# Twelve of 48 weight pieces narrowed after the last scores instead of among them: a talking-heads attention with two expert layers on one core

## The chip, the cores and the metric

One core of one Trainium2 chip runs the whole program in one launch. The metric is device time in microseconds (us) of that launch. Of several runs the median counts; a difference of about 1% is what a measurement of this kernel can tell from none.

The engines are named as the profile names them: PE is TensorE (PEld its weight loads), DVE is VectorE, ACT is ScalarE, POOL is GpSimd, SP is SyncE, which here only issues DMAs. A "q" behind an engine's name is that engine's queue of instructions.

## The reference

An attention with mixed heads (4 batches, 12 heads, 448 positions, 64 wide), followed by two feed-forward layers over its 1792 tokens:

```python
scores = scale * np.matmul(q, k.transpose(0, 1, 3, 2))
scores = np.einsum('bhij,hg->bgij', scores, w_pre)
attn = softmax(scores)                      # row maximum taken off, sum + 1e-9
attn = np.einsum('bhij,hg->bgij', attn, w_post)
x = np.matmul(attn, v)                      # (B, H, S, D) -> (1792, 768)

h = x @ w_in                                # 768 x 1024
solu = h * softmax(h)
x = (layernorm(solu) * g_ln) @ w_out        # 1024 x 768

r = np.maximum(x @ w2_in, 0.0)              # 768 x 2048
out = (r * r) @ w2_out                      # 2048 x 768
```

The four weight matrices reach the kernel as 64-bit floats. The kernel narrows them to 32 bits itself: it takes two 32-bit words of each number, shifts and joins their bits, and zeroes what is too small for 32 bits. All further arithmetic is in 32 bits; the feed-forward products are made of three matmuls each on a high and a low part of every operand.

## The kernel before

**The attention in passes.** The queries are cut into 16 chunks (120, 120, 120 and 88 rows of each batch), and the chunks into 180 blocks of up to ten query rows. A loop over passes `s` (line 573, here from -5 to 91) handles two blocks at a time, and its stages are spread over neighbouring passes. Pass `s` issues the shuffles of pair `s+5` (line 220: DMAs on SP that bring all heads' scores of a block under each other), `pre(s+2)` (line 240: PE mixes the heads), `negmax` and `expo` of pair `s+2` (line 251 on DVE, 258 on ACT), `weigh(s+1)` (lines 268 to 271, three POOL instructions that divide the second mixing weights by the row sums) and `post(s)` (line 297: PE mixes again; it needs `weigh(s)`). `qk` (line 206) makes the scores of a later chunk, at most two heads' pairs a pass, until pass 79, which the code calls `last_qk`. `av` (line 336) multiplies a finished chunk by v, in 32 calls; the last three fall into pass 90. The order of the instructions on every engine's queue is the order of this loop: the schedule is written out by hand, and no queue overtakes.

**The first weights during the attention.** `w1pieces` (line 380) lists 48 pieces of 128 by 256 numbers: 24 of `w_in`, then 24 of `w_out`, three for each 128 rows. For one piece there is a load of 256 KB on POOL's queue (line 386), a square on ACT (80), three bit operations on DVE (83, 87, 91; `filler()` runs them, seven at a time, in passes with an `av`), a comparison and a product on POOL (100, 101), for `w_out` a scaling by `g_ln` on ACT (407) and a store of 128 KB on SP (412) into the DRAM tiles `w1iD` and `w1oD`. The pace is a budget of bytes (lines 565 to 591): what pieces, k, q, v and results move is spread evenly from pass 5 to pass 64. When all pieces are through (pass 75 by this bookkeeping), the pool `raws` closes and `wi1` opens.

**The end of the attention.** `prep_first` (line 418) brings the first layer's operands in: a load on SP (433, 438), a cast on ACT (444) and a subtraction on POOL (445) make the two parts of a block; a load runs two steps ahead of its cast, in three buffers. It takes three steps when `wi1` opens, one each in passes 80 to 84 and two each from pass 85; its last splits are in pass 88. At pass 79 the pools of q and k (`early`) and of the even chunks' scores are closed, and `wi1b` opens in their place. `h1(0)`, the first product of the first layer (line 457), begins in passes 88 and 89 and ends in pass 90 behind the last `av`. In pass 90 the last results go out by DMAs on ACT's queue (line 370).

**The first layer.** For each of 14 tiles of 128 tokens: `h1(m)` on PE, `norm1(m)` on DVE, ACT and POOL (lines 713 to 739), then `zt(m)`, PE's transposes of its result (line 753), and `out1` (767). `load_w1_out` (687) reads `w1oD` two blocks of 128 rows per tile in the first four tiles; the split casts on ACT and subtracts on POOL (692, 693). From the fourth tile on a generator, `w2stream` (line 788), narrows the second weights in another manner: a square on ACT (806), one POOL instruction that makes a mask (807), and three bit operations on DVE (831, 835, 837).

Of the kernel before, what the change touches and what calls it, by code (L numbers as in the profile page):

```python
# [7 lines left out]
F32 = mybir.dt.float32  # L8
F32R = mybir.dt.float32r
U32 = mybir.dt.uint32  # L10
I64 = mybir.dt.int64
AF = mybir.ActivationFunctionType
ALU = mybir.AluOpType
# [5 lines left out]
def kernel(  # L19
# [16 lines left out]
    nc = tc.nc  # L36
    B, D, _ = qT.shape
# [15 lines left out]
    scale = 1.0 / float(D) ** 0.5  # L53
# [19 lines left out]
    g_sb = const.tile([128, F1 // 128], F32, name="g_sb")  # L73
# [42 lines left out]
    raws = tc.tile_pool(name="raws", bufs=1, side="left", reuse_waits="tile")  # L116
# [35 lines left out]
    NP = NB // 2  # L152
# [222 lines left out]
    WP = 256  # L375
    w1raw = {}
    w1f = {}
    w1s = {}
    w1t = {}
    w1pieces = [(w1_in, w1iD, k, o) for k in range(CC) for o in range(0, F1, WP)]  # L380
    w1pieces += [(w1_out, w1oD, k, o) for k in range(F1 // 128) for o in range(0, DM, WP)]

    def load_w1(i):
        src, dst, k, o = w1pieces[i]
        t = raw_p.tile([128, WP], I64, tag="w1raw", name="w1raw", bufs=7)
        nc.gpsimd.dma_start(out=t, in_=src[k * 128:(k + 1) * 128, o:o + WP])
        w1raw[i] = t
# [22 lines left out]
    def store_w1(i):  # L410
        src, dst, k, o = w1pieces[i]
        nc.sync.dma_start(out=dst[k * 128:(k + 1) * 128, o:o + WP], in_=w1t.pop(i))

    w1i = []
    xs = {}
# [51 lines left out]
    def run(part):  # L467
        for _ in part:
            pass
# [72 lines left out]
    for c, ch in enumerate(chunks):  # L542
        if c:
            beg = (chunks[c - 1]["first"] + 1) // 2 - DS
            end = ch["first"] // 2 - DS
            for p in range(HP):
                rest = end - beg >= HP
                s = beg + rest + p * (end - beg - rest) // HP
# [13 lines left out]
    last_qk = max(s for s, js in jobs.items() for f, a in js if f is qk)  # L562
    w1at = []
    kept = 0
    kb = {load_k: 448, load_v: 384, load_q: 360, x_out: 360}
    moved = {s: sum(kb.get(f, 0) for f, a in js) for s, js in jobs.items()}
    first_w1, last_w1 = 5, 64
    share = (384 * len(w1pieces) + sum(moved.get(s, 0) for s in range(first_w1, last_w1))) / (last_w1 - first_w1)
    room = owed = begun = 0
    last_raw = None  # L570
    at_slot(2, load_const)
    lo_s = min(min(jobs), -DS)
    for s in range(lo_s, NP + 2):
# [8 lines left out]
        ready = sorted(w1t)  # L582
# [3 lines left out]
                f(*a)  # L586
        if first_w1 <= s:
            room += share - moved.get(s, 0)
        while room >= 384 and owed < len(w1pieces):
            room -= 384  # L590
            owed += 1
        for _ in range(2):
# [28 lines left out]
        for i in sorted(w1f):  # L621
            sq, t = w1f.pop(i)
# [10 lines left out]
        for i in ready:  # L633
            store_w1(i)
        kept = begun - len(fill)
        if last_raw is None and kept == len(w1pieces) and not w1t and not w1s and not w1f:
            last_raw = s
            assert s < last_qk, s
            raws.__exit__(None, None, None)
            wi1 = tc.tile_pool(name="wi1", bufs=1, side="left", reuse_waits="tile")  # L640
            wi1_p = wi1.__enter__()
            half_line(wi1_p)
            prep = prep_first()
        if s == last_qk:
            early.__exit__(None, None, None)
            sspools[0].__exit__(None, None, None)
            wi1b = tc.tile_pool(name="wi1b", bufs=1, side="left", reuse_waits="tile")
            wi1b_p = wi1b.__enter__()
        if s + DP == NP - 1:
            psb.__exit__(None, None, None)  # L650
            psh = tc.tile_pool(name="psh", bufs=1, side="left", space=PSUM, reuse_waits="tile")
            psh_p = psh.__enter__()
            h10 = h1(0)
# [8 lines left out]
        if s == NP:  # L662
            run(prep)
            run(h10)
    assert not jobs

    psa.__exit__(None, None, None)
    sspools[1].__exit__(None, None, None)
# [432 lines left out]
    low = []  # L1101
# [168 lines left out]
    for q in range(NQ):  # L1270
        p = q // NE
# [6 lines left out]
        for k, x in enumerate(seq):  # L1278
# [8 lines left out]
            if parts:  # L1287
                t, c = parts[0]
                if q == NE - 1 and (t[1] in ("p2", "p4") or t[1] in ("p7", "p3") and k < 7):
                    t = None  # L1290
                if t:
                    parts.pop(0)
                    split_xc(*t, c)
                    i = ORDER.index(t[1]) + 2
# [76 lines left out]
```

## Time and profile before

| | us |
|---|---|
| three runs | 1110.02, 1102.11, 1110.64 |
| median | 1110.02 |
| the profiled execution | 1105.38 |
| its span, first to last instruction | 1103.60 |

The span is cut into 40 slices, and a digit is the busy share of a slice in tenths. The attention fills the first 14 slices (to about 395 us), the first layer the next nine, the second the rest.

```profile
PE   7889888988899899999999999999999999999998
PEld 3556555655656687989999998999999999999998
DVE  2556666877685626788887526677656843444444
ACT  4556556767676726444443446444334655444432
POOL 2746788897684836665564338666535766666630
PEclk8899899999999999999999999999999999999999
DMA  6868778788676634565754736455455431111102
```

A wait is read as "who waited <- for whom: us in total, times, longest"; "issue" is idle time in which the engine waited for nothing that the profile shows. The clock column is the granted TensorE clock as a share of full speed, DMA the busy share of the core's 16 DMA engines.

### The profile page before, as it was taken

How to read it: one execution, taken by the hardware profiler on the slowest of the kernel's cores; microseconds unless marked ns; L12 is line 12 of the kernel's file. 1: busy time of each engine (PE TensorE's matmuls, PEld its weight loads, DVE VectorE, ACT ScalarE, POOL GpSimd, SP SyncE). 2: the span in 40 equal slices, each digit the busy share in tenths (PEclk: the TensorE clock that was granted, in tenths of full speed). 3: DMA queues.
4: the chain of work that ended last, by engine and by line, in shares of the span. 5: the costliest groups of instructions: out<-in, count | busy, mean ns of one | idle time of the engine just before them, and what ended most of it. 6: DMA issues, size and time to landing. Idle time of an engine off the chain costs nothing.

```text
span 1103.6 us, 30919 instructions
## 1 busy us (share of the span) xinstructions
PE 1043.0 (95%) x12560; PEld 890.0 (81%) x12560; DVE 680.4 (62%) x1217; ACT 562.0 (51%) x1171; POOL 673.4 (61%) x872
## 2 busy tenths in 40 slices
PE   7889888988899899999999999999999999999998
PEld 3556555655656687989999998999999999999998
DVE  2556666877685626788887526677656843444444
ACT  4556556767676726444443446444334655444432
POOL 2746788897684836665564338666535766666630
PEclk8899899999999999999999999999999999999999
DMA  6868778788676634565754736455455431111102
GB/s 176 212 179 239 207 220 260 219 259 244 202 225 196 180 99 127 166 195 167 210 159 158 229 120 181 135 157 172 143 200 192 161 129 58 58 58 58 58 29 100
DMA packets 115918, 180.33 MB, mean 163 GB/s; under 512 B 24224, under 2 KB 87328, under 8 KB 115776
## 3 DMA queue, kind: packets, MB, share of 16 engines
q1 hardware_dynamic: 100788, 128.66, 38.1%
q0 software_dynamic: 12608, 47.77, 14.5%
q10 hardware_dynamic: 2380, 1.93, 0.6%
q8 instruction: 99, 1.62, 0.6%
q14 instruction: 43, 0.35, 0.1%
HBM read 101.63 MB, written 38.14 MB: 127 GB/s over the span
## 4 chain that ended last, share of the span: by engine, by line
PE 73%; issue 7%; DMA 7%; POOL 6%; ACT 4%; DVE 4%; SPq 0%; ACTq 0%; POOLq 0%; DVEq 0%
PE ps_y L1184 19%; PE ps_h L1113 16%; PE ps_o L767 9%; PE ps_h L457 7%; PE ps_ring L336 6%; PE ps_ring L297 6%; PE ps_pre L240 5%; PE ps_ring L206 5%; DMA sdst<-ssrc 3%; ACT ssrc L213 1%; POOL ti L1041 1%; DMA ra<-w2iD 1%; DMA wraw<-w1iD 1%; ACT e L258 1%; DMA w2oD<-nt 1%
## 5 line engine op out<-in xcount | busy, mean ns | idle before, releaser
L1184 PE MATMUL ps_y<-to,gt 128*128 128x384 f32 x1332 | 241.9, 336 | 2.5 <-POOL to L1049 1.8
L1184 PEld LDWEIGHTS ps_y<-to,gt 128*128 128x128 f32 x1332 | 233.7, 188 | 4.8 <-POOL to L1049 2.1
L1113 PE MATMUL ps_h<-xc,ti 128*128 128x448 f32 x1080 | 225.1, 362 | 0.6 <-ACT h L1129 0.6
L1113 PEld LDWEIGHTS ps_h<-xc,ti 128*128 128x128 f32 x1080 | 201.6, 187 | 13.2 <-ACT h L1129 1.0
L297 PEld LDWEIGHTS ps_ring<-w,e 60*64 60x64 f32 (+1 forms) x5760 | 101.9, 137 | 70.8 <-issue 42.4
L316 DVE COPY at<-ps_ring 128x420 f32<-128x420 f32 x156 | 87.8, 611 | 94.9 <-PE ps_ring L297 94.7
L1195 DVE TENSOR_TENSOR y<-ps_y,y 128x768 f32<-128x768 f32 x97 | 92.3, 954 | 76.9 <-PE ps_y L1184 76.5
L807 POOL TENSOR_SCALAR nt<-nt 128x256 f32<-128x256 f32 x96 | 112.0, 1166 | 43.9 <-ACT nt L806 37.8
L297 PE MATMUL ps_ring<-w,e 60*64 60x60 f32 (+2 forms) x5760 | 110.3, 221 | 29.8 <-issue 23.9
L213 ACT COPY ssrc<-ps_ring 128x896 f32<-128x896 f32 x92 | 82.1, 908 | 95.7 <-PE ps_ring L206 88.8
L258 ACT ACTIVATE e<-ps_pre,nm 128x448 f32<-128x448 f32 x180 | 113.3, 640 | 23.3 <-DVE nm L251 23.1
L767 PE MATMUL ps_o<-zt,w1o 128*128 128x384 f32 (+1 forms) x720 | 120.7, 326 | 1.4 <-ACT o L775 1.2
L457 PE MATMUL ps_h<-w1i,xs 128*128 128x512 f32 x504 | 118.1, 391 | 0.7 <-POOL xs L707 0.6
L767 PEld LDWEIGHTS ps_o<-zt,w1o 128*128 128x128 f32 x720 | 116.9, 189 | 2.1 <-ACT o L775 1.6
L251 DVE TENSOR_REDUCE nm<-ps_pre 128x1 f32<-128x448 f32 x180 | 102.9, 611 | 16.9 <-PE ps_pre L240 16.9
L457 PEld LDWEIGHTS ps_h<-w1i,xs 128*128 128x128 f32 x504 | 93.9, 188 | 20.3 <-POOL xs L707 1.5
L1041 POOL TENSOR_TENSOR ti<-ra,ti 128x384 fp32r<-128x384 f32 x56 | 60.2, 1083 | 78.3 <-ACT ti L1040 77.9
L1126 DVE TENSOR_TENSOR gt<-h,gt 128x448 fp32r<-128x448 f32 x64 | 50.6, 790 | 90.2 <-ACT gt L1131 85.5
L206 PE MATMUL ps_ring<-k,q 64*64 64x448 f32 x752 | 98.3, 560 | 6.8 <-ACT ssrc L213 2.9
L240 PE MATMUL ps_pre<-sdst,wpre_bd 64*64 64x448 f32 (+1 forms) x720 | 97.8, 575 | 6.7 <-issue 5.5
L806 ACT ACTIVATE nt<-nraw 128x256 f32<-128x256 f32 x96 | 40.7, 432 | 121.6 <-DMA w2iD<-nt 47.8
L336 PEld LDWEIGHTS ps_ring<-at,v 128*64 128x64 f32 x1536 | 77.0, 140 | 31.6 <-PE ps_pre L240 9.9
(108 smaller groups left out, 1474.0 us busy)
## 6 DMA issues: line engine op xcount, KB each, us to landing
sdst<-ssrc SPq DMA_DIRECT2D x166, 210.0 KB
nraw<-in_moe_w_in_dram SPq DMA_DIRECT2D x48, 256.0 KB
nraw<-in_moe_w_out_dram SPq DMA_DIRECT2D x48, 256.0 KB
ra<-w2iD POOLq DMA_DIRECT2D x32, 384.0 KB, 4.4
ro<-w2oD POOLq DMA_DIRECT2D x32, 384.0 KB, 4.0
w1raw<-in_moe_w_in_dram POOLq DMA_DIRECT2D x24, 256.0 KB, 6.0
w1raw<-in_moe_w_out_dram POOLq DMA_DIRECT2D x24, 256.0 KB, 6.3
w2iD<-nt SPq DMA_DIRECT2D x48, 128.0 KB
```

The costliest lines, as they stand in the source:

```text
L206: nc.tensor.matmul(out=ps[64 * u:64 * u + 64, e, 0:S], lhsT=qq[c][64 * e:64 * e + 64, p * n + u * half:p * n + u * half + 64], rhs=k[64 * ...
L213: (nc.vector.tensor_copy if dve else nc.scalar.copy)(ssrc[c][:, p:H:HP, :], ps[:, :, 0:S])
L240: nc.tensor.matmul(out=ps[b][64 * u:64 * u + 64, 0:S], lhsT=wpre_bd[64 * r:64 * r + m], rhs=ds[b][64 * r:64 * r + m], start=True, stop=True,)
L251: nc.vector.tensor_reduce(out=nm, in_=pres[s][b][:, 0:S], op=ALU.max, axis=AX.X, negate=True)
L258: nc.scalar.activation(out=e, in_=pres[s][b][:, 0:S], func=AF.Exp, bias=nms.pop((s, b)), scale=1.0, accum_out=sms[s][:, b:b + 1])
L297: nc.tensor.matmul(out=ps[64 * c:64 * c + 64, u, i0:i0 + ng * RH], lhsT=e[64 * u:64 * u + m, o:o + 64], rhs=w[64 * u:64 * u + m, b, g0:g0 ...
L336: nc.tensor.matmul(out=ps[64 * e:64 * e + 64, 0, q * 120:q * 120 + n], lhsT=t[:, g] if j < NJ else t[:, e, p], rhs=at[c][:, j * H + (g if ...
L457: nc.tensor.matmul(out=ps[:, u], lhsT=t[:, a, cc], rhs=w1i[cc][:, w, u * 512:(u + 1) * 512], start=(cc == 0 and a == 0 and w == 0), stop=( ...
L767: nc.tensor.matmul(out=ps[:, 0:width], lhsT=w1o[k][:, w, cc * 128:(cc + 1) * 128], rhs=zT[:, a, k, 0:width], start=(k == 0 and i == 0), st ...
L807: nc.gpsimd.tensor_scalar(out=t, in0=t, scalar1=2.0**-30, scalar2=2.0 - 2.0**-23, op0=ALU.is_ge, op1=ALU.mult)
L1113: nc.tensor.matmul(out=bank[b][:, 0:HT], lhsT=t[:, w, c], rhs=xc[xn][:, a, c], start=(first and j == 0 and c == 0 and i == 0), stop=(j == ...
L1184: nc.tensor.matmul(out=ps[:, u - u2[0], 0:DM // 2], lhsT=gt[:, a, f, o:o + 128], rhs=w[:, v, f, u * (DM // 2):(u + 1) * (DM // 2)], start= ...
```

## The change

The budget of the attention's passes counts 36 pieces (`NW`) instead of 48; it still ends at pass 64, so the 36 are spread over the same passes. The other twelve, all of `w_out` (the last four blocks of 128 rows), are narrowed by a generator, `tail_w1`, in a pool of its own that opens behind `wi1b` at pass 79. The generator takes one step in each pass from 80 to 89, four in pass 90, one in pass 91 and the rest behind the loop, always before the step of `prep_first` of the same pass. Its first step issues four loads, its second two masks; each of the twelve steps after that issues the load four pieces on, the mask two pieces on, the three bit operations of one piece, and the scaling and the store of the piece before. It narrows in the manner of `w2stream`; loads and stores are both on SP. With fewer pieces `raws` closes at pass 72 instead of 75.

```diff
+    NW = len(w1pieces) - 12
...
+        def load(i):
+            if i in todo:
+                src, dst, k, o = w1pieces[i]
+                raws[i] = pool.tile([128, WP], I64, tag="traw", name="traw", bufs=5)
+                nc.sync.dma_start(out=raws[i], in_=src[k * 128:(k + 1) * 128, o:o + WP])
...
+        def mask(i):
+            if i in todo:
+                t = ts[i] = pool.tile([128, WP], F32, tag="tt", name="tt", bufs=6)
+                nc.scalar.activation(out=t, in_=words(i)[1].bitcast(F32), func=AF.Square)
+                nc.gpsimd.tensor_scalar(
+                    out=t, in0=t, scalar1=2.0**-30, scalar2=2.0 - 2.0**-23, op0=ALU.is_ge, op1=ALU.mult
+                )
+
+        def scaled():
+            for i in ready:
+                k = w1pieces[i][2]
+                nc.scalar.activation(out=ts[i], in_=ts[i], func=AF.Copy, scale=g_sb[:, k:k + 1])
+
+        def store():
+            while ready:
+                i = ready.pop(0)
+                src, dst, k, o = w1pieces[i]
+                nc.sync.dma_start(out=dst[k * 128:(k + 1) * 128, o:o + WP], in_=ts.pop(i))
+
+        a = todo[0]
+        for i in range(4):
+            load(a + i)
+        yield True
+        mask(a)
+        mask(a + 1)
+        yield True
+        for i in todo:
+            load(i + 4)
+            mask(i + 2)
+            low, high = words(i)
+            bits = ts[i].bitcast(U32)
+            stt = nc.vector.scalar_tensor_tensor
+            stt(out=bits, in0=high, scalar=3, in1=bits, op0=ALU.logical_shift_left, op1=ALU.bitwise_and)
+            scaled()
+            stt(out=bits, in0=high, scalar=0xC0000000, in1=bits, op0=ALU.bitwise_and, op1=ALU.bitwise_or)
+            stt(out=bits, in0=low, scalar=29, in1=bits, op0=ALU.logical_shift_right, op1=ALU.bitwise_or)
+            store()
+            raws.pop(i)
+            ready.append(i)
+            yield True
+        scaled()
+        store()
...
-    share = (384 * len(w1pieces) + sum(moved.get(s, 0) for s in range(first_w1, last_w1))) / (last_w1 - first_w1)
+    share = (384 * NW + sum(moved.get(s, 0) for s in range(first_w1, last_w1))) / (last_w1 - first_w1)
...
-        if last_raw is None and kept == len(w1pieces) and not w1t and not w1s and not w1f:
+        if last_raw is None and kept == NW and not w1t and not w1s and not w1f:
...
             wi1b_p = wi1b.__enter__()
+            tail = tc.tile_pool(name="tail", bufs=1, side="left", reuse_waits="tile")
+            tail_steps = tail_w1(tail.__enter__())
+        elif s > last_qk:
+            for _ in range(4 if s == NP else 1):
+                next(tail_steps, None)
...
     assert not jobs
+    run(tail_steps)
+    tail.__exit__(None, None, None)
```

## Rows read from the trace of the kernel before

**Rows 1.** Busy time in four stretches; columns: PE, PEld, DVE, ACT, POOL, clock, DMA, GB/s.

```profile
60.00:300.00 240.00, 207.80 (x5366) 137.50 (x5360) 164.93 (x357) 155.75 (x367) 183.50 (x330) 0.97 0.78 228
300.00:345.00 45.00, 40.02 (x1110) 28.05 (x1108) 32.99 (x74) 33.00 (x82) 33.25 (x61) 1.00 0.69 200
345.00:376.00 31.00, 29.72 (x908) 21.31 (x906) 19.69 (x39) 21.64 (x51) 18.74 (x32) 1.00 0.67 196
376.00:395.00 19.00, 15.87 (x409) 12.76 (x402) 9.95 (x22) 9.86 (x22) 16.88 (x22) 0.91 0.58 170
```

**Rows 2.** Waits of PE, 60 to 300 us: us in total, times, longest.

```profile
PE ps_ring L297 <- issue: 17.9, 13, 3.1
PE ps_pre L240 <- issue: 5.5, 2, 3.3
```

**Rows 3.** Waits of PE, 300 to 345 us.

```profile
PE ps_ring L297 <- issue: 3.0, 2, 2.0
```

**Rows 4.** Timeline of PE, one stop inside a group of line 297.

```profile
336.99 1.08 PE L297 MATMUL ps_ring<-w,e 60*64 60x60 f32 x58
340.09 0.31 PE L297 MATMUL ps_ring<-w,e 60*64 60x30 f32 x6 [2.02 <-issue]
```

**Rows 5.** DMA queues, 337.5 to 338.9 us: packets, MB, share.

```profile
q8 instruction: 1, 0.02, 4.2%
```

**Rows 6.** Waits of PE, 345 to 376 us.

```profile
PE ps_ring L297 <- POOL w L271: 0.7, 1, 0.7
PE ps_ring L297 <- issue: 0.4, 1, 0.4
```

**Rows 7.** Waits of PE, 376 to 395 us.

```profile
PE ps_ring L297 <- issue: 1.9, 1, 1.9
PE ps_ring L297 <- POOL w L271: 1.3, 2, 0.7
```

**Rows 8.** Timeline where the attention ends; the releaser stands in brackets.

```profile
392.35 0.39 POOL L271 TENSOR_TENSOR w<-wpost_bd,sm 128x120 f32<-128x120 f32 x1
...
392.79 1.13 PE L297 MATMUL ps_ring<-w,e 60*64 60x60 f32 x64 [0.51 <-POOL w L271]
...
403.89 2.02 ACTq L370 DMA_DIRECT2D xD<-xt  x3
406.09 1.23 DVE L717 TENSOR_REDUCE nm<-ps_h 128x1 f32<-128x1024 f32 x1 [10.94 <-PE ps_h L457]
...
414.25 0.86 PEld L753 LDWEIGHTS ps_tr<-id_sb,e 128*128 128x128 f32 x8 [0.46 <-ACT e L738]
```

**Rows 9.** Groups of the whole trace: both narrowings, of the first and second weights.

```profile
L807 POOL TENSOR_SCALAR nt<-nt 128x256 f32<-128x256 f32 x96 | 112.0, 1166 | 43.9 <-ACT nt L806 37.8
...
L835 DVE SCALAR_TENSOR_TENSOR nt<-nraw,nt 128x256 uint32<-128x256 uint32 x96 | 64.4, 671 | 2.5
...
L837 DVE SCALAR_TENSOR_TENSOR nt<-nraw,nt 128x256 uint32<-128x256 uint32 x96 | 51.6, 537 | 2.8
...
L831 DVE SCALAR_TENSOR_TENSOR nt<-nraw,nt 128x256 uint32<-128x256 uint32 x96 | 44.8, 467 | 7.6 <-POOL nt L807 7.6
L100 POOL TENSOR_SCALAR w1sq<-w1sq 128x256 f32<-128x256 f32 x48 | 41.3, 860 | 4.1
L806 ACT ACTIVATE nt<-nraw 128x256 f32<-128x256 f32 x96 | 40.7, 432 | 121.6 <-DMA w2iD<-nt 47.8 <-DMA w2oD<-nt 33.6 <-DVE nt L837 11.3
...
L101 POOL TENSOR_TENSOR w1t<-w1t,w1sq 128x256 f32<-128x256 f32 x48 | 35.0, 729 | 4.0
```

**Rows 10.** The splits on POOL at the attention's end, 361 to 395.3 us: busy, mean ns | idle before.

```profile
L445 POOL TENSOR_TENSOR w1i<-wraw,w1i 128x512 fp32r<-128x512 f32 x12 | 15.2, 1276 | 2.9 <-ACT w1i L444 1.5 <-DMA sdst<-ssrc 0.9 <-DMA wraw<-w1iD 0.5
```

**Rows 11.** Timeline of SP's queue in the passes after the last scores.

```profile
362.10 1.33 SPq L433 DMA_DIRECT2D wraw<-w1iD  x1
```

**Rows 12.** The page's DMA issues: KB each, us from issue to landing.

```profile
ra<-w2iD POOLq DMA_DIRECT2D x32, 384.0 KB, 4.4
...
w1raw<-in_moe_w_out_dram POOLq DMA_DIRECT2D x24, 256.0 KB, 6.3
```

More of the change, by code (lines that the diff above doesn't have):

```diff
@@ L412, in store_w1, with tail_w1, words @@
         nc.sync.dma_start(out=dst[k * 128:(k + 1) * 128, o:o + WP], in_=w1t.pop(i))
+    def tail_w1(pool):
+        todo = range(NW, len(w1pieces))
+        raws, ts, ready = {}, {}, []
+        def load(i):
[3 more added lines that the diff above has]
+                nc.sync.dma_start(out=raws[i], in_=src[k * 128:(k + 1) * 128, o:o + WP])
+        def words(i):
+            pair = raws[i].bitcast(U32).rearrange("p (n two) -> p n two", two=2)
+            return pair[:, :, 0], pair[:, :, 1]
+        def mask(i):
[37 more added lines that the diff above has]
+        store()
     w1i = []
@@ L588 @@
             room += share - moved.get(s, 0)
-        while room >= 384 and owed < len(w1pieces):
+        while room >= 384 and owed < NW:
             room -= 384
```

## The prediction, made before the change was run

> **What bounds the kernel now.** I read the page first, then the busy times by stretch, the waits of PE stretch by stretch, the chain of waits, and the timeline from the last scores to the first layer. Up to 345 us the attention and the first weights run together; from 345 us the weights are through; at 376 us the passes with two splits each begin [rows 1]. From 60 to 345 us PE is idle for 32.2 + 5.0 = 37.2 of 285 us [rows 1], and most of that is "issue": 23.4 us before 300 us in the two largest rows [rows 2] and 3.0 us behind it [rows 3], 26.4 together. These are stops inside a group: 58 of the 64 matmuls of one `post` start, then nothing for two microseconds, then the last six [rows 4]. In that stop the instruction queue moves one packet of 16 KB [rows 5], and the other long stops have such a packet too. So I read them as PE's own instructions arriving late, among data that keeps the DMA engines 78% busy [rows 1].
>
> Behind 345 us it looks otherwise. With the DMA engines 67% busy such stops cost 0.4 us in 31 us [rows 1, 6]. From 376 us on POOL is busy for 16.88 of 19 us, more than PE [rows 1], and PE waits for `weigh` as well as for issue [rows 7]: the last `post` starts right after POOL's last `weigh` [rows 8]. POOL alternates `weigh`, which the next `post` needs, with the splits. The end of the attention is thus POOL's, and everything earlier is PE's with stops.
>
> **What the attention's passes get back.** Twelve pieces fewer are a quarter of the first weights: 12 x 384 KB = 4.7 MB of the 240 x 228 + 45 x 200 = 63.7 MB that move from 60 to 345 us [rows 1], and on POOL 12 x (0.86 + 0.73) = 19 us [rows 9], beside their loads' issue. POOL, DVE and ACT have idle time there, and hardly a wait of PE for them is long, so what counts is PE's idle time. Issue costs 23.4 / 240 = 0.098 us per us before 300 us, 3.0 / 45 = 0.067 while the last pieces drain, and (0.4 + 1.9) / 50 = 0.046 with no first weights [rows 1 to 3, 6, 7]. By the last of these the first weights cause 26.4 - 0.046 x 285 = 13.3 us, and a quarter is 3.3; by the middle one 26.4 - 0.067 x 285 = 7.3, a quarter 1.8; if all of it were theirs, 6.6. I take 3.5. Of PE's other idle time, 37.2 - 26.4 = 10.8 us, a quarter would be 2.7; I take 2. Sum: 5.5 us back, bounds 1.8 and 9.3.
>
> A rule of the Trainium skill speaks against the larger part. "Runtime: NRT & Kernel Launch", section "Instruction fetch mechanics", says that instructions come in 16 KB blocks by a DMA queue of their own, and that this is hidden because dispatch is slower than the refill. The block size agrees with rows 5; that it is hidden doesn't agree with the stop in rows 4. By the rule 3.5 of the 5.5 us would fall away, which is the third rival.
>
> **What the end of the attention pays on POOL.** The new masks are the instruction of line 807, 1.17 us each [rows 9]; with a gap of 0.08 us ahead of each, as POOL's old comparisons had (4.1 us idle over 48) [rows 9], 1.25 us. Two are issued in pass 81, one in each of passes 82 to 87, all ahead of `weigh(89)`, the last that `post` waits for: 8 x 1.25 = 10.0 us. What can hide them is POOL's idle time ahead of the splits, 2.9 us [rows 10], so the bounds are 7.1 and 10.0. Part of that idle time is a wait for ACT's casts, which also get work, and 0.9 us of it falls into pass 80, before any mask. I take 8.5. The masks of pieces 8 and 9 come behind `weigh(89)` and delay the last splits, which `h1(0)` needs only after 6 us of `av`: nothing.
>
> **On the other queues.** DVE's three operations, 0.47 + 0.67 + 0.54 = 1.67 us a piece [rows 9], fit into its idle time (it is busy for 19.69 of 31 and 9.95 of 19 us) [rows 1]; so does ACT's square of 0.43 and one scaling. SP gets twelve loads and twelve stores. The first four loads stand ahead of pass 80's `prep_first` load and pass 81's shuffles; one load issue took 1.33 us [rows 11], so the shuffles are some 5 us later. They have three passes until `pre` needs them, and by then POOL's masks have moved `pre` back as far: I take nothing, bounds 0 and 2. A store waits for its scaling on ACT, and the loads of `prep_first` queue behind it; that is the second rival. New traffic also brings back stops of PE; much of that falls into waits for POOL. I take 1.0, bounds 0 and 3.
>
> **What the first layer pays.** In pass 90 the masks of pieces 10 and 11 are queued behind the last copies and four DMA issues on ACT, which end at 403.89 + 2.02 = 405.9 us [rows 8]. From there, on the old clock: square 0.43 (406.4), mask 1.17 and a gap (407.6), three DVE operations of piece 10 (409.3), and of piece 11 (411.0), whose mask is ready by then. All these are queued ahead of the row maximum of `norm1(0)`, which started at 406.09, the moment that `h1(0)` was done [rows 8]. It comes 4.9 us later. PE makes `h1(1)` meanwhile, but that cover is used up already: `zt(0)` waited 0.46 us for the end of `norm1(0)` [rows 8]. From there on PE has no pause to catch up in. I take 4.9, bounds 3.2 (one piece's 1.67 us less, if DVE has done piece 10 by then) and 6.1 (one more mask of 1.17 in the way). The first layer's tiles may lie where the new pool was and wait for its last stores; the trace of before can't show that: 0, at most 4 by the nearest landing of 4.4 us [rows 12].
>
> **Sum.** Against the profiled execution, 1105.4: -5.5 + 8.5 + 1.0 + 4.9 = +8.9, so 1114.3. That execution lies 4.6 us under the median of the runs, which spread over 8.5 us, and 3.3 over the fastest. I stay close to the sum and forecast 1115 us: slightly slower, by less than the 1% (11 us) that a measurement of this kernel can tell from no change.
>
> **The rivals.**
> First, the stops vanish out of proportion and the change is no loss. For it: with 67% busy DMA engines they were nearly gone, 0.4 / 31 = 0.013 per us [rows 1, 6]. 4.7 of 63.7 MB are 7.4%, which takes 78% to 72%, or 0.06 of the 0.11 on the way to 67%: 55% of 23.4 - 0.013 x 240 = 20.3 us, so 11.2, with 2.7 of the other waits 13.9 back. POOL hides the 2.9 it can (7.1), the first layer pays 4.9: 1105.4 - 13.9 + 7.1 + 4.9 = 1103.5. It decides from about 13 us back. Against it: from 300 to 345 us the engines were 69% busy and stops cost 0.067 all the same.
>
> Second, SP and the DMA engines take over at the end, and the kernel is slower for certain. From 361 to 395 us about 15 x 196 + 19 x 170 = 6.2 MB move [rows 1]; twelve loads and seven stores add 4.0. At the 228 GB/s of the loaded stretch [rows 1] 10.2 MB want 45 us, where the old 34 us and POOL's 8.5 make 42.5. A load of 256 KB took 6.3 us to land in the loaded stretch, against 4.4 us for 384 KB later [rows 12], 2 us more. In passes 85 to 88 ACT's casts wait for such loads with the next exponentials behind them: 4 x 2 = 8 us on top, 1122.3. PE, waiting longer, may also be granted less clock; it was 0.91 there already [rows 1]. Against it: the pieces' traffic is spread over more passes than these four.
>
> Third, the stops are not of the traffic but of PE's own dense groups, and don't change; only 1 or 2 us of other waits come back. Then 1105.4 - 2 + 8.5 + 1.0 + 4.9 = 1117.8. For it: in the last 19 us, with 58% busy DMA engines and no first weights, they cost 1.9 / 19 = 0.10 per us again [rows 1, 7]. The rule of the skill named above would make it so as well, by another road. Against it: a fall from 0.098 to 0.013 as the pieces end.
>
> **How the numbers follow.** The forecast gets 0.45 (1108 to 1120), the first rival 0.20 (1097 to 1107), the second 0.18 (1120 to 1130), the third 0.17 (1114 to 1122). The range is 1100 to 1126: it leaves out the lower end of the first rival and the upper half of the second, under 0.2 together. Slower by over 1%, from 1121 us: 0.15 of the second, 0.07 of the third, 0.08 of the forecast, as the runs may lie above a profile by as much as they did before: 0.30. Faster by over 1%, under 1099 us: 0.08, all of the first. Within 1%: 0.62.
>
> **What would show it.** In the profile after: PE's waits for issue from 60 to 345 us fall from 26.4 to some 23 us and the passes to pass 80 end 5 or 6 us sooner; behind it POOL is busy without a gap, PE's waits for `weigh` rise from 2.0 to about 8 us, the last `post` stands 2 to 5 us later than 392.79; the row maximum of `norm1(0)` starts some 5 us after the end of `h1(0)`, its releaser a tail operation on DVE, and `zt(0)` waits as long. From then on both kernels keep step. Wrong would be: `weigh` not last at the end of the attention (then SP, DMA or nothing is), stops of PE down by more than a third or unchanged, or `norm1(0)` starting with `h1(0)`'s end.

## The result: slower by about 1%, with the profile after

The change makes the kernel slower: 1119.51 us in the median of six runs (1117.60 to 1127.92) against 1109.99 in six of the kernel before beside them. The medians differ by 9.5 us; the ratio on record for these runs is 1.0111 with a 95% interval of 1.0067 to 1.0155, which is some 12 us (7.4 to 17.2). The forecast was 1115 in a range of 1100 to 1126; the sign and the range hold, and the loss lies on the border between "same" and "slower" at 1%.

The execution that was profiled after took 1122.39 us (span 1120.6), 17.0 more than the one profiled before, so this pair lies further apart than the medians. First the busy times by stretch, with the columns of [rows 1]; the last stretch ends later, as the attention does:

```profile
60.00:300.00 240.00, 208.87 (x5366) 141.34 (x5364) 155.01 (x327) 148.90 (x348) 163.90 (x302) 0.96 0.74 212
300.00:345.00 45.00, 40.37 (x1085) 28.26 (x1080) 29.69 (x67) 29.92 (x73) 27.22 (x53) 0.96 0.71 206
345.00:376.00 31.00, 25.60 (x780) 18.30 (x780) 19.92 (x40) 22.02 (x53) 17.16 (x27) 0.97 0.60 181
376.00:408.00 32.00, 23.71 (x564) 18.61 (x558) 24.98 (x43) 16.61 (x40) 29.35 (x36) 0.82 0.66 199
```

Up to 345 us the removed work is plain to see on POOL (163.90 us for 183.50 in the first stretch) and in the traffic (212 GB/s for 228), but PE is busy hardly longer, 208.87 us for 207.80. From 345 us PE loses: 25.60 of 31 us for 29.72 [rows 1]. Then POOL is busy for 29.35 of 32 us.

Second, whom PE waited for, from 60 to 345 us, to be held against [rows 2, 3]:

```profile
PE ps_ring L297 <- issue: 12.2, 12, 3.1
PE ps_pre L240 <- issue: 8.8, 3, 3.6
PE ps_ring L206 <- issue: 4.8, 2, 2.6
PE ps_ring L336 <- issue: 3.8, 2, 3.4
```

These are 29.6 us; all of PE's issue waits in the same stretch of before were 28.8 (the prediction's 26.4 is the rows of [rows 2, 3] alone). This one execution gave nothing back. From 345 to 408 us, where before had 2.0 us of waits for `weigh` [rows 6, 7]:

```profile
PE ps_ring L297 <- POOL w L271: 4.1, 1, 4.1
...
PE ps_ring L297 <- POOL w L271: 7.0, 2, 4.6
PE ps_ring L297 <- DVE at L316: 1.3, 1, 1.3
```

POOL's groups from 361 to 408 us show what was added: the splits of [rows 10] are the same in number and nearly in length (1.32 us for 1.28), and the masks stand beside them.

```profile
L504 POOL TENSOR_TENSOR w1i<-wraw,w1i 128x512 fp32r<-128x512 f32 x12 | 15.6, 1315 | 1.6 <-ACT w1i L503 1.0
L434 POOL TENSOR_SCALAR tt<-tt 128x256 f32<-128x256 f32 x9 | 10.0, 1106 | 2.8 <-ACT tt L433 1.3 <-DMA traw<-in_moe_w_out_dram 1.0
```

Last, the timeline where the attention ends, with the events of [rows 8] (in after the row maximum is line 783 and the transposes are line 819):

```profile
406.04 1.13 PE L297 MATMUL ps_ring<-w,e 60*64 60x60 f32 x64
...
417.15 2.00 ACTq L370 DMA_DIRECT2D xD<-xt  x3
...
419.20 0.43 ACT L433 ACTIVATE tt<-traw 128x256 f32<-128x256 f32 x1 [2.15 <-issue]
...
419.72 2.46 POOL L434 TENSOR_SCALAR tt<-tt 128x256 f32<-128x256 f32 x2 [9.38 <-ACT tt L433]
...
423.13 0.42 DVE L465 SCALAR_TENSOR_TENSOR tt<-traw,tt 128x256 uint32<-128x256 uint32 x1
...
423.47 1.22 DVE L783 TENSOR_REDUCE nm<-ps_h 128x1 f32<-128x1024 f32 x1
...
431.70 1.25 PEld L819 LDWEIGHTS ps_tr<-id_sb,e 128*128 128x128 f32 x8 [4.66 <-ACT e L804]
```

The last `post` starts at 406.04 for 392.79, 13.3 us later. `h1(0)` is done at 419.3, but the row maximum waits for the tail's last bit operation, until 423.47, and the transposes wait 4.66 us for 0.46. From the first transposes to the last instruction both kernels take the same: 688.9 us after, 689.4 before. So the 17.0 us are: 1.1 up to pass 79 (its row maximum starts at 359.3 for 358.2), 12.1 from there to the last `post`, 4.2 at the first layer, and 0.4 less in the rest.

### The profile page after: what moved, and what is told of

Its sections match the earlier page's. It is cut to its first block, busy times and chain, and to the rows that moved or that the text cites. A ratio compares the mean times of both kernels' runs of the same rounds, so it can differ in the third digit from the quotient of the medians.

```text
span 1120.6 us, 30899 instructions
## 1 busy us (share of the span) xinstructions
PE 1050.3 (94%) x12560; PEld 898.4 (80%) x12560; DVE 686.9 (61%) x1217; ACT 562.9 (50%) x1171; POOL 663.4 (59%) x848
## 3 DMA queue, kind: packets, MB, share of 16 engines
q0 software_dynamic: 11648, 44.62, 13.3%
q10 hardware_dynamic: 2380, 1.93, 0.6%
## 4 chain that ended last, share of the span: by engine, by line
PE 51%; POOL 4%; issue 3%; DMA 2%; DVE 1%; ACT 1%; ACTq 0%; SPq 0%; POOLq 0%
PE ps_y L1250 18%; PE ps_h L1179 15%; PE ps_o L833 10%; PE ps_h L516 7%; POOL ti L1107 1%; DMA ra<-w2iD 1%; PE ps_tr L819 1%; POOL w1o L759 1%; POOL s L1087 1%; DMA nraw<-in_moe_w_in_dram 1%; POOL to L1115 1%; DVE st L792 0%; DVE e L789 0%; DMA w1oraw<-w1oD 0%; ACT e L786 0%
## 5 line engine op out<-in xcount | busy, mean ns | idle before, releaser
L297 PEld LDWEIGHTS ps_ring<-w,e 60*64 60x64 f32 (+1 forms) x5760 | 104.4, 140 | 70.4 <-issue 32.2
L873 POOL TENSOR_SCALAR nt<-nt 128x256 f32<-128x256 f32 x96 | 112.1, 1168 | 42.1 <-ACT nt L872 36.1
L516 PE MATMUL ps_h<-w1i,xs 128*128 128x512 f32 x504 | 120.5, 397 | 0.0
L240 PE MATMUL ps_pre<-sdst,wpre_bd 64*64 64x448 f32 (+1 forms) x720 | 102.6, 583 | 9.7 <-issue 8.8
```

The costliest lines, as they stand in the source:

```text
L240: nc.tensor.matmul(out=ps[b][64 * u:64 * u + 64, 0:S], lhsT=wpre_bd[64 * r:64 * r + m], rhs=ds[b][64 * r:64 * r + m], start=True, stop=True,)
L297: nc.tensor.matmul(out=ps[64 * c:64 * c + 64, u, i0:i0 + ng * RH], lhsT=e[64 * u:64 * u + m, o:o + 64], rhs=w[64 * u:64 * u + m, b, g0:g0 ...
L516: nc.tensor.matmul(out=ps[:, u], lhsT=t[:, a, cc], rhs=w1i[cc][:, w, u * 512:(u + 1) * 512], start=(cc == 0 and a == 0 and w == 0), stop=( ...
L873: nc.gpsimd.tensor_scalar(out=t, in0=t, scalar1=2.0**-30, scalar2=2.0 - 2.0**-23, op0=ALU.is_ge, op1=ALU.mult)
```

## The experiments

One table for all of them. "To pass 79" is the start of that pass's row maximum; "end" is from there to the last `post`; "late" is by how much the row maximum of `norm1(0)` starts behind the end of `h1(0)`; "stops" are all issue waits of PE from 60 to 345 us. These four are of one profiled execution each. The ratio to the kernel before, with its interval, is the one on record for the runs beside it; it differs a little from the quotient of the medians, which is 1.0086 for after.

```
kernel                         to pass 79   end   late  stops  ratio [95%]
before                              358.2  34.6   0.0   28.8   1
before, a second profile            357.6  35.7   0.0   30.6
before, a third profile             355.1  33.5   0.0   27.9
after                               359.3  46.7   4.2   29.6   1.0111 [1.0067, 1.0155]
e1  tail left out                   351.4  36.1   0.0   21.4   0.9926 [0.9892, 0.9961]
e2  36 pieces left out              353.9  34.8   0.0   25.1   0.9912 [0.9874, 0.9949]
e3  masks on DVE                    356.9  43.1   3.5   20.2   1.0050 [1.0021, 1.0078]
e4  last pieces a pass sooner       358.3  45.7   0.1   32.0   1.0064 [1.0029, 1.0098]
e5  transfers alone, shared buffers 356.9  50.6   0.0   28.4   1.0110 [1.0072, 1.0148]
e6  arithmetic alone                357.8  46.2   4.4   20.6   1.0087 [1.0059, 1.0115]
e9  transfers alone                 355.5  43.7   0.0   25.1   0.9987 [0.9948, 1.0026]
e8  reordered, masks on POOL        354.6  43.9   0.1   27.1   1.0049 [1.0022, 1.0077]
e7  reordered, masks on DVE         354.6  40.2   0.0   26.2   1.0013 [0.9980, 1.0046]
e10 as e7, last pieces before av    351.7  41.6   0.0   23.2   0.9967 [0.9934, 1.0000]
```

PE's time in the end is either its own work or a wait. The second table parts it, from the busy times and PE's waits in that stretch of the same profiles; the work is the same in all of them. "Shuffles" are waits of line 240 for the shuffles' DMAs, "others" are waits for issue, ACT and DVE, "clock" is the mean granted TensorE clock.

```
kernel                               end   busy  weigh  shuffles  others  clock
before                              34.6   30.2    1.9       0      2.3   0.95
before, a second profile            35.7   31.1    4.4       0      0.2   0.95
before, a third profile             33.5   28.0    5.5       0      0     1.00
after                               46.7   33.0   11.1       0      2.6   0.85
e1  tail left out                   36.1   30.5    5.6       0      0     0.91
e2  36 pieces left out              34.8   29.9    3.7       0      1.3   0.95
e3  masks on DVE                    43.1   34.0    9.2       0      0     0.84
e4  last pieces a pass sooner       45.7   32.2   13.5       0      0     0.85
e5  transfers alone, shared buffers 50.6   37.7    7.9       4.7    0.2   0.83
e6  arithmetic alone                46.2   33.9    6.2       0      6.0   0.85
e9  transfers alone                 43.7   33.6    5.7       3.0    1.2   0.88
e8  reordered, masks on POOL        43.9   32.9    8.6       2.3    0     0.88
e7  reordered, masks on DVE         40.2   31.8    3.9       2.4    2.0   0.92
e10 as e7, last pieces before av    41.6   32.1    6.2       2.5    0.8   0.92
```

From e1 to after the end grows by 10.6 us: 5.5 in waits for `weigh`, 2.6 in other waits, and 2.5 in PE's own work, which runs at a lower clock.

My theory was the prediction's: the masks on POOL make the end longer, the queue order of pass 90 makes the first layer late, and the attention's passes give a few microseconds back. The rivals were that SP and the DMA engines make the end longer, and that PE's stops have nothing to do with the pieces.

**The tail left out (e1).** Edit: the generator is never made, so twelve pieces are not narrowed at all, and the first layer reads the blocks that are there.

```diff
-            tail = tc.tile_pool(name="tail", bufs=1, side="left", reuse_waits="tile")
-            tail_steps = tail_w1(tail.__enter__())
-        elif s > last_qk:
-            for _ in range(4 if s == NP else 1):
-                next(tail_steps, None)
```

> The twelve last pieces are left out altogether (36 are narrowed; the first layer's last four weight blocks are read from the first four). What the attention's passes get back by themselves is then seen without the tail. If the stops of PE don't follow the pieces (the trace of the changed kernel: waits for issue from 60 to 300 us 25.4 us against 25.2 before): the row maximum of pass 79 stands at 358 +- 3 us, the last post at 393 +- 3, and the time is within 3 us of the kernel before. If the prediction's sum was right and the one profile was an unlucky one: pass 79 some 5 us sooner than 358, and 1104 to 1106 us against 1110.

Measured: 0.9926 (0.9892 to 0.9961), 8.2 us under before (4.3 to 12). The end takes 36.1 us, against 33.5 to 35.7 in the three profiles of before, and nothing is late. Pass 79 stands at 351.4, 6.8 us sooner than in the first profile of before: of the two branches expected it is the second, and further than it said. So nearly all of the longer end and all of the late first layer are the tail's.

**A quarter of the pieces (e2).** As e1, and 24 more pieces are left out of the attention's passes.

```diff
-    NW = len(w1pieces) - 12
+    NW = len(w1pieces) - 36
```

> Only the first twelve of 48 pieces are narrowed in the attention, no tail; 36 pieces are left out, and the first layer reads blocks that are there. If PE's stops come of the first weights' traffic: waits for issue from 60 to 345 us fall from 29 us to 10 or less, and the kernel is 15 to 20 us faster than before. If they are PE's own: they stay above 20 us, and the kernel is faster by 5 us or less, by the waits for POOL, DVE and ACT alone.

Measured: the same time as e1 within the intervals, 0.9912 (0.9874 to 0.9949), or 9.8 us under before (5.7 to 14). From 60 to 345 us it has less traffic and much less work on POOL (columns of [rows 1]):

```profile
60.00:345.00 285.00, 251.68 (x6632) 169.33 (x6628) 161.15 (x327) 171.36 (x393) 140.34 (x288) 0.97 0.65 181
```

Before, by the same view, the DMA engines were busy for 0.76 at 223 GB/s and POOL for 216.75 us. Yet the stops are there still:

```profile
PE ps_ring L297 <- issue: 19.9, 13, 4.4
PE ps_ring L336 <- issue: 4.1, 4, 2.1
```

With one more of 1.1 that is 25.1 us. The stops stay above 20 us, but the gain is more than the "5 us or less" expected for that case. They don't follow the traffic down; with it at 0.65, just under the 0.67 [rows 1] at which they cost 0.4 us in 31 [rows 6], they cost 25.1 us in 285.

**Before, twice more (b1, b2).** No edit; two more profiles of the kernel before, to see how far the stops scatter.

> The kernel before, unchanged, for a second profile of its attention passes. Ten profiles of kernels with 36 pieces there have the row maximum of pass 79 between 351.4 and 359.3 us, 355.7 in the mean; the one profile with 48 has 358.2. If 36 pieces give back what the medians say (7 us without a tail): 358 to 366, with waits for issue from 60 to 345 us as scattered as in the others (20 to 32 us). If the pieces give nothing back and the medians come from elsewhere: 352 to 359.

> The kernel before once more, a third profile, with the same two expectations: 358 to 366 if the twelve pieces cost the attention's passes some 7 us, 352 to 359 if they cost nothing.

Measured: 30.6 and 27.9 us of stops, pass 79 at 357.6 and 355.1. With 48 pieces the three profiles have 29.1 us of stops on the mean. Ten kernels have 36 pieces in the attention's passes and the same instructions there; their profiles run from 20.2 to 32.0 us, 25.4 on the mean, and pass 79 from 351.4 to 359.3, on the mean 355.7 for 357.0 with 48. Both new profiles fall into the branch by which the pieces give nothing back. But a single profile can't show a gain of four microseconds here; the profile of after was among the worst of the ten. The three profiled executions of before were also quick ones, 1104.8 us on the mean, some 4 us under that kernel's medians (1108.1 to 1110.0), while the ten lay 1.5 us over the medians of theirs. With these 5.6 us added to the 1.3, pass 79 would come some 7 us sooner; this is an estimate, and it takes the whole scatter to lie ahead of pass 79.

The kept traces also say what the stops hang on. In the 14 profiles PE has 261 issue waits from 60 to 345 us, and all 261 end 1.15 to 1.9 us after the end of a packet of the instruction queue q8; the one of [rows 4] ends 1.4 us after it. Of all moments in that stretch 14% lie so, and of PE's 220 other waits 39. So I read the stops as PE waiting for its instructions, though no run varied that alone. The traffic of data does not show in the packets: there are 52 of them in that stretch of before and 53 in e2, with a median of 1.06 us each in both.

**Masks on DVE (e3).** POOL loses the masks, DVE gains them, all else stays.

```diff
-                nc.gpsimd.tensor_scalar(
-                    out=t, in0=t, scalar1=2.0**-30, scalar2=2.0 - 2.0**-23, op0=ALU.is_ge, op1=ALU.mult
-                )
...
+            nc.vector.tensor_scalar(
+                out=ts[i], in0=ts[i], scalar1=2.0**-30, scalar2=2.0 - 2.0**-23, op0=ALU.is_ge, op1=ALU.mult
+            )
```

> As the changed kernel, but the twelve masks are made by DVE just ahead of the bit operations instead of by POOL. If POOL's masks ahead of weigh are what the end of the attention pays: PE's waits for weigh behind 345 us fall from 11 us to 4 or less, the last post stands 6 to 9 us sooner than the 406 of the changed kernel, and the time is 6 to 9 us below it. If it is the landing of the new loads and the queue on SP and ACT: no more than 2 us.

Measured: 1.0050 (1.0021 to 1.0078), and an end of 43.1 us. On DVE a mask takes 0.41 us instead of 1.1 (group of line 459 in this kernel, 355 to 412 us):

```profile
L459 DVE TENSOR_SCALAR tt<-tt 128x256 f32<-128x256 f32 x10 | 4.1, 414 | 0.0
```

Of the 10.6 us that the tail adds to the end of e1, only 3.6 went with POOL's masks, and the median fell by 4.3 us where 6 to 9 were expected. PE still waits for `weigh`, POOL in its turn waits for ACT's casts, and those wait for the first layer's loads. The waits of PE, POOL and ACT from 358 to 407 us:

```profile
PE ps_ring L297 <- POOL w L271: 9.2, 3, 3.7
...
POOL w1i L504 <- ACT w1i L503: 6.7, 3, 3.2
...
ACT w1i L503 <- DMA wraw<-w1iD: 7.8, 5, 4.2
```

Before, that last wait was 4.4 us in the same stretch, and in e1, without a tail, 6.5; so the loads' landing by itself explains little. ACT is also busier, 28.2 us of the end for 22.0 in e1, with the tail's squares and scalings. There is a cause beside POOL's masks; this run does not say which.

**The last pieces a pass sooner (e4).** Three steps in pass 89 and two in pass 90, so that the last squares and masks don't stand behind pass 90's results.

```diff
-            for _ in range(4 if s == NP else 1):
+            for _ in range(2 if s == NP else 3 if s == NP - 1 else 1):
```

> As the changed kernel, but three steps of the tail are taken in pass 89 and two in pass 90, so that the last two squares stand ahead of the last copies and result DMAs on ACT. If the order of ACT's queue in pass 90 is what makes the first layer start late: the row maximum of norm1(0) starts within 0.5 us of the end of h1(0) (4.2 us behind it in the changed kernel), and the time is 3 to 5 us below the changed kernel's, less what two masks earlier on POOL cost. If the rest of the tail's work on DVE is what is late: no change.

Measured: 1.0064 (1.0029 to 1.0098). The row maximum starts with the end of `h1(0)` and the transposes wait 0.55 us, as before the change:

```profile
416.36 2.02 ACTq L370 DMA_DIRECT2D xD<-xt  x3
...
418.64 1.23 DVE L783 TENSOR_REDUCE nm<-ps_h 128x1 f32<-128x1024 f32 x1 [4.58 <-PE ps_h L516]
...
426.81 0.86 PEld L819 LDWEIGHTS ps_tr<-id_sb,e 128*128 128x128 f32 x8 [0.55 <-ACT e L804]
```

The gain is not the whole 4.2 us: the last `av` now waits 1.0 us for DVE, which has the earlier bit operations in its queue, and from the last `post` to the end of `h1(0)` it takes 14.5 us instead of 13.3. The median fell by 3.8 us; the intervals overlap, so the row shows it and the medians only agree. The end stays long, at 45.7 us.

**The arithmetic alone (e6).** No load and no store of the tail; its squares, masks, bit operations and scalings run on a tile of zeros, and the result goes nowhere.

```diff
-        for i in range(4):
-            load(a + i)
+        raw = pool.tile([128, WP], I64, name="traw")
+        nc.vector.memset(raw.bitcast(F32), 0.0)
+        for i in todo:
+            raws[i] = raw
```

> As the changed kernel, but the tail moves no data: squares, masks, bit operations and scalings work on one zeroed tile, and loads and stores of the twelve pieces are left out. From the row maximum of pass 79 to the last post: by POOL's ledger 34.6 or 36.1 plus 7 to 10, so 43 to 46; if the transfers are the cost, 38 or less. The first layer still starts 4 us late (norm1(0) behind the end of h1(0)), as those two squares stand where they stood.

Measured: an end of 46.2 us, 10.1 more than e1, with the DMA engines busy for only 0.46 of it. The arithmetic by itself makes nearly the whole longer end. The POOL group of the masks within that end:

```profile
L434 POOL TENSOR_SCALAR tt<-tt 128x256 f32<-128x256 f32 x9 | 9.8, 1084 | 0.8 <-DMA sdst<-ssrc 0.2
```

Nine masks keep POOL busy for 9.8 us, about as long. But the run takes the squares, scalings and bit operations along, so it prices all the arithmetic and not POOL's share alone: PE's waits for `weigh` are only 6.2 us here, 4.4 are put down to ACT, and ACT's exponentials wait 10.1 us for DVE's row maxima, where e1 has 4.5. e8 and e7 below part the masks from the rest.

**The transfers alone (e5, then e9).** e5 has the tail's loads and stores and no arithmetic, but stores straight out of the loads' buffers.

```diff
+        def plain(i):
+            src, dst, k, o = w1pieces[i]
+            nc.sync.dma_start(out=dst[k * 128:(k + 1) * 128, o:o + WP], in_=raws.pop(i).bitcast(F32)[:, 0:WP])
```

> As the changed kernel, but the tail only moves data: each of the twelve pieces is loaded and its first words are stored, with no instruction of the tail on ACT, DVE or POOL (the narrowing of these pieces is left out). Measure: from the row maximum of pass 79 to the last post, 34.6 us in the kernel before, 36.1 without a tail, 46.7 in the changed kernel. If POOL's masks and the waits that they make are the cost: 37 or less. If the transfers on SP and the DMA engines are: 43 or more, and ACT's waits for the loads of the first layer's weights at 7 us or more. Both in part: 38 to 42.

Measured: an end of 50.6 us, longer than after itself. That came from the experiment: a later load needs the buffer of an earlier store, and SP's queue stood still for it with the first layer's loads behind. The waits of SP's queue and of ACT, 355 to 410 us:

```profile
SPq L424 <- DMA w1oD<-traw: 20.5, 6, 4.9
...
ACT w1i L495 <- DMA wraw<-w1iD: 24.8, 10, 6.9
```

So it does not price the transfers of the change. e9 stores from a tile of zeros instead, so that no load waits for a store:

```diff
+        zero = pool.tile([128, WP], F32, name="tz")
+        nc.vector.memset(zero, 0.0)
...
+            nc.sync.dma_start(out=dst[k * 128:(k + 1) * 128, o:o + WP], in_=zero)
```

> The transfers alone once more: the twelve loads as in the change, and twelve stores of a tile of zeros, so that no load waits for a store and no store for a load (the narrowing of the twelve pieces is left out). From the row maximum of pass 79 to the last post: 36.1 us without a tail, 46.1 with its arithmetic alone, 46.7 with both. If the transfers cost nothing where POOL is last: 36 to 38, and 1100 to 1104 us. If they alone cost as much as the arithmetic does, each hiding the other: 43 or more. By the run with the masks on DVE (43.2 with the transfers) I expect 39 to 42.

Measured: an end of 43.7 us, 7.6 more than e1, where 39 to 42 was expected; it meets the branch "43 or more". Waits of PE, POOL and ACT, 355 to 410 us:

```profile
PE ps_ring L297 <- POOL w L271: 5.7, 3, 3.9
PE ps_pre L240 <- DMA sdst<-ssrc: 3.0, 2, 2.5
PE ps_ring L297 <- issue: 1.2, 1, 1.2
...
POOL w1i L499 <- ACT w1i L498: 9.2, 7, 3.7
...
ACT w1i L498 <- DMA wraw<-w1iD: 14.3, 10, 3.3
```

The second rival's chain is there: ACT's casts wait 14.3 us for their loads and POOL 9.2 for the casts, where e1 has 6.5 and 2.4. But it does not reach PE, whose waits for `weigh` are no longer than in e1:

```profile
PE ps_ring L297 <- POOL w L271: 5.6, 4, 3.1
```

What PE loses is 3.0 us of waits for the shuffles, which share SP's queue and the DMA engines with the new transfers, 1.2 of a stop, and 3.1 in its own work, at a mean clock of 0.88 for 0.91. Arithmetic 10.1 and transfers 7.6 give 10.6 together: each hides most of the other. That fits e3, which got only 3.6 us back.

**Reordered (e8, e7).** All work is done. The tail's step stands behind the step of `prep_first`, a store comes a step later than before, a scaling at the end of its step, squares a pass later, and the last pieces are spread over passes 88 to 90 (2, 3 and 2 steps). e8 leaves the masks on POOL, e7 has them on DVE.

```diff
-        elif s > last_qk:
-            for _ in range(4 if s == NP else 1):
-                next(tail_steps, None)
...
+            for _ in range({NP - 2: 2, NP - 1: 3, NP: 2}.get(s, 1)):
+                next(tail_steps, None)
```

> As the run before it, but the masks on POOL again, as in the change. If POOL's masks count by themselves: 3 to 8 us more than that run, on the way from pass 79 to the last post. If the order of the loads and stores was the whole cost: the same within 2 us.

> All twelve pieces done, but arranged by what the runs so far say: masks on DVE, the tail's step behind that of the first layer's operands in each pass, the squares a pass later than the first loads, a store a step behind its scaling, and two, three and two pieces in passes 88, 89 and 90, where ACT, DVE and POOL wait for PE. If the cost of the tail is where it stands in the queues: from pass 79 to the last post 37 to 40 us, norm1(0) within 1 us of the end of h1(0), and 1101 to 1106 us, below the kernel before (1108.1) and the changed one. If moving 4 MB there costs the same whatever the order: 43 us or more and 1110 or more.

Measured: ends of 43.9 and 40.2 us, nothing late, ratios of 1.0049 (1.0022 to 1.0077) and 1.0013 (0.9980 to 1.0046). The two differ in the masks' engine alone: 3.7 us of the end, 1.9 us behind the last `post`, and 4.8 us of the medians. PE's waits for `weigh` from 355 to 410 us, e8 first, then e7:

```profile
PE ps_ring L297 <- POOL w L271: 8.6, 4, 4.4
```

```profile
PE ps_ring L297 <- POOL w L271: 3.9, 2, 2.2
...
PE ps_ring L336 <- DVE at L321: 1.8, 1, 1.8
```

In e7 the last `av` waits 1.8 us for DVE, which has bit operations in its queue: from the last `post` to the end of `h1(0)` it takes 15.3 us instead of 13.3. In e8 it takes 17.2: the last `av` waits 2.0 us, and its last 96 matmuls then take 5.51 us for 3.86.

**The last pieces before the last av (e10).** As e7, but the steps of pass 90 stand ahead of the last `av` calls, and POOL, idle there, makes the last five scalings, with their stores behind the loop; the masks' tile gets a seventh buffer.

```diff
+        for _ in range(4 if s == NP else 0):
+            next(tail_steps, None)
         for f, a in js:
...
-            for _ in range({NP - 2: 2, NP - 1: 3, NP: 2}.get(s, 1)):
+            for _ in range({NP - 2: 2, NP: 0}.get(s, 1)):
```

> All twelve pieces done. As the run with the masks on DVE and the later steps, but only one piece in pass 89, and four in pass 90 ahead of the last av calls, so that no bit operation stands ahead of the last post_out; the last five scalings go to POOL, which is idle there. If DVE ahead of post_out was what that run still lost behind the last post (15.3 us to the end of h1(0), 13.3 in the kernel before): 13.3 again, and 2 us less in all, 1106 to 1108 us. If the last copies and the first norm meet the four pieces on DVE and ACT again: no less than that run's 1109.5.

Measured: 0.9967 (0.9934 to 1.0000), 1107.83 us. The stretch behind the last `post` is back at 13.3 us. It is the best version that does all the work, but at most 0.7% better than before and at the edge of none: what the attention's passes give back is about what the tail, well placed, still costs.

## Why the prediction was right, and where it failed

**What bounds the kernel: right.** POOL decides the end of the attention; after the change PE waits there for `weigh` for 11.1 us instead of 2.0, and for nothing else longer than 1.3. Without a tail that wait is 1.9 to 5.6 us in five profiles, so not all of the rise is the change's. POOL was forecast to be busy without a gap; it is busy for 29.35 of the last 32 us.

**The attention's passes, 5.5 us back: not contradicted, not settled.** It was made of 3.5 from the stops and 2 from other waits. In the one profile after there was nothing, and stops unchanged were a sign of being wrong that the prediction named itself. Over all profiles the first twelve pieces taken away bring the stops from 29.1 to 25.4 us, 3.7; pass 79 comes only 1.3 us sooner on the mean (357.0 to 355.7), some 7 by the estimate above, and e1's ratio puts that kernel 8.2 us (4.3 to 12) under before. Of the reason given, one half holds and one failed. By the traces the stops are instructions arriving late: all of them end shortly behind an instruction packet. But the data's traffic is not what makes most of them: e2, with another 24 pieces gone, has 25.1 us. The third rival, that they don't change with the traffic, describes those 25 us better; why the packets come late, and why the sum differs so from one execution to the next, is open. "Runtime: NRT & Kernel Launch", section "Instruction fetch mechanics", of the Trainium skill says that the refill of instructions is hidden. These traces don't agree with it: from 60 to 345 us they have 20.2 to 32.0 us of stops that end behind such a refill. The first rival, stops that vanish out of proportion, is refuted by e2.

**POOL's masks, 8.5 us: the mechanism right, the size not settled.** All the tail's arithmetic makes 10.1 us in e6, the upper bound, and the masks there keep POOL busy for 9.8. In after a mask took 1.11 us, where 1.17 was taken. Where only the masks' engine is changed, the end loses 3.7 us from e8 to e7 and 3.6 from after to e3, since other causes then come last: the 10.1 is what the arithmetic costs by itself, not what taking the masks off POOL brings.

**SP and the DMA engines, nothing (0 to 2): right on top of the masks, for a reason that failed.** From e6 to after, the transfers add 0.6 us to the end. But they are not harmless by themselves: e9 shows 7.6 us. The prediction gave the shuffles three passes of time, and in after PE does not wait for them; in e9 it does, for 3.0 us. The second rival had about the size, 8 us, but not the way: its wait for the first layer's loads does not lengthen PE's waits for `weigh` in e9, and it was wrong to add the 8 us to POOL's masks. The sum came out nearly right in part by luck: a cost was taken as nothing, and another term covered it.

**The end in all: 9.5 us forecast (8.5 and 1.0 for new stops), 12.1 measured,** or 10.6 against e1. One part of what is left over is in ACT's waits from 361 to 408 us: the squares waited for the tail's own loads, which the sum did not have.

```profile
ACT tt L433 <- DMA traw<-in_moe_w_out_dram: 2.9, 2, 1.7
```

Another is PE's own work, 2.8 us longer in the end than before at a mean clock of 0.85 for 0.95, told below.

**The first layer, 4.9 us: right, 4.2 measured,** by the chain that was forecast: the copies' DMAs end at 419.15, the square starts at 419.20, the masks end at 422.2, the bits at 423.55, and the row maximum stands behind them. e4 took this away, and paid 1.2 us of it ahead of `h1(0)`.

**"Then both kernels keep step": right,** 688.9 against 689.4 us.

**The total.** 1115 was forecast and 1119.5 measured. The last `post` was to be 2 to 5 us late and was 13.3: 5.5 us of gain did not come in that execution, and the end was 2.6 us dearer. That the sum, 8.9 us, agrees with the 9.5 between the medians is partly luck. e1 splits the change into a gain of 8.2 us, where 5.5 was forecast, and a price, from e1 to after, of 18.8 by the medians, where 8.5, 1.0 and 4.9 make 14.4: both were taken too small. One gap stays open: of that price the profiles' segments show 10.6 and 4.2. Single profiles scatter by as much as the rest, so I don't put a cause to it.

## What to carry to other kernels

Work moved out of a loaded stretch is paid for where it lands: list, queue by queue, what stands ahead of the instruction that is last there, and sum it up. Here that forecast the late first layer within a microsecond and the longer end 2.6 us too short. Price the moved arithmetic and the moved transfers separately, each with the other taken away, since two causes that run side by side hide each other, and removing one then brings little. Where the waits to be saved differ by ten microseconds between executions, judge by medians of many runs or by several profiles.

## What the runs showed of the hardware that was not expected

The granted TensorE clock fell right after PE had waited for POOL. Four stretches of after, with the columns of [rows 1]:

```profile
376.00:382.00 6.00, 6.00 (x92) 4.60 (x85) 4.43 (x7) 1.49 (x5) 5.40 (x8) 0.59 0.83 244
382.00:388.00 6.00, 3.84 (x150) 2.53 (x146) 4.55 (x9) 4.98 (x12) 5.34 (x7) 1.00 0.66 201
...
400.00:406.00 6.00, 6.00 (x76) 4.82 (x72) 3.41 (x7) 3.00 (x7) 5.59 (x7) 0.60 0.54 184
406.00:412.00 6.00, 6.00 (x115) 5.16 (x116) 4.34 (x10) 0.25 (x1) 4.17 (x4) 1.00 0.12 41
```

The means 0.59 and 0.60 lie between the two levels, 1.2 and 2.4 GHz, near the lower. PE's timeline shows what came before, and that the work was slower:

```profile
374.95 1.93 PE L297 MATMUL ps_ring<-w,e 60*64 60x60 f32 x64 [4.08 <-POOL w L271]
...
378.36 3.89 PE L336 MATMUL ps_ring<-at,v 128*64 128x120 f32 x48
382.18 1.13 PE L297 MATMUL ps_ring<-w,e 60*64 60x60 f32 x64
...
399.79 1.45 PE L297 MATMUL ps_ring<-w,e 60*64 60x60 f32 x44 [4.57 <-POOL w L271]
```

After 4.08 us without work the 64 matmuls of a `post` took 1.93 us, and 1.13 at full clock a few microseconds later; the second fall came after a pause of 4.57 us, and its 64 matmuls took 1.93 us too (the last row is cut off at 401 us). The length of the pause alone doesn't decide it: in e6 a pause of 2.36 us was followed by 1.93 us for such a group, in e3 one of 3.09 us by 1.13. In the whole end PE was busy for 33.0 us in after and 30.5 in e1 with the same 868 matmuls, so up to 2.5 us of the longer end are in its slower work. How much of that reached the end of the attention, where POOL was last for the most part, no run here tells apart.

The second finding is what PE's stops hang on, the packets of its instruction queue, and how unequal executions of the same instructions are: 20.2 to 32.0 us of stops in ten profiles of the same attention passes.
